# Linear attention into a tanh-shrink layer: inputs laid out as (head group, 64) x 9 tokens, q transposed by DMA, 1/den of batches 0 and 1 spread by fp32 matmuls, phi two batches ahead

## Chip, cores and metric

The kernel runs on one NeuronCore of one Trainium2 chip. The metric is the device time of one execution in microseconds (us); the median of three runs of the kernel before is 398.22 us (397.93 to 398.74). One execution was also recorded by the hardware profiler.

## What is computed

Shapes: q, k, v are (8 batches, 8 heads, 576 tokens, 64); the layer behind is 512 to 2048 to 512 over 4608 tokens.

```python
def _attn_ref(q, k, v):
    def phi(x):
        return np.where(x > 0, x, np.exp(x) - 1.0) + 1.0
    q_p, k_p = (phi(q), phi(k))
    kv = np.einsum('bhsd,bhse->bhde', k_p, v)
    z = np.sum(k_p, axis=2)
    num = np.einsum('bhsd,bhde->bhse', q_p, kv)
    den = np.einsum('bhsd,bhd->bhs', q_p, z)[..., None] + 1e-06
    return (num / den).astype(np.float32)

def _moe_ref(x, w_in, w_out):
    h = x @ w_in
    g = h - np.tanh(h)
    return (g @ w_out).astype(np.float32)
```

The attention output, laid out as 4608 tokens x 512, is the x of the second function.

## The kernel before

Everything is written in the order in which each engine is to run it (a manual schedule); engines wait for each other through semaphores only. Matmuls take bf16 operands; q, k, v and the weights are cast to bf16 by the loading DMAs, which GpSimd (POOL) issues.

The second layer is cut into nine **chunks** c of 512 tokens. In a chunk, L1 is sixteen calls of `l1` (4 matmuls of 512 columns into one PSUM bank h, a tanh on ScalarE (ACT), h - tanh(h) into gT on VectorE (DVE)); L2 is sixteen calls of `l2mm` (4 matmuls each into a bank o), and after every fourth an `evac` copies o to SBUF on ACT and SP stores it. `s1[fi]` and `s2[s]` are lists of attention steps that are emitted behind L1 step fi and L2 step s of a chunk; what stands there sets the order on all engines.

The attention of a **batch** has these steps. `a_kphi` and `a_qphi`: exp on ACT, max(x,0)+1 and the min of the two on DVE (tiles e, r, kp, qp). The 576 tokens lie as 512 (128 partitions x 4) and a rest of 64 with tiles of its own (km and kraw, qm and qraw, vm and vr), so phi runs twice. `a_qT`: twenty 128x128 transposes on TensorE (PE), four copies on ACT. `a_kv`: twenty matmuls of 192 columns, masked into kz by DVE. `a_den`: sixteen matmuls of 144 columns, then a reciprocal rden on DVE; rden goes to DRAM (ds) by four DMAs and comes back, copied to 64 partitions per head, as rdb by two more, all issued by SP. `a_num`: eight matmuls in five PSUM tiles, each multiplied by rdb on DVE into xT, the operand of L1.

`attention(0)` runs ahead of chunk 0 and `attention(1)` behind it, step after step, with no chunk beside them. From chunk 1 on, chunk c carries kv, den and num of batch c+1 (den at `s1[13]`, num from `s2[9]`) and phi and the transposes of batch c+2 (phi at `s2[0]` and `s2[1]`, transposes from `s2[3]`); chunk 1 carries phi and transposes of batch 2 as well. PSUM has six banks for h and o (pool dps) and two for all of attention (pool aps).

Of the kernel before, what the change touches and what calls it, by code (L numbers as in the profile page):

```python
# [15 lines left out]
def kernel(  # L16
# [51 lines left out]
    def load_k(b):
        km = kpool.tile([128, H, J, D], BF16, name="km")
        nc.gpsimd.dma_start(out=km.rearrange("p h j d -> p h (j d)"),  # L70
                            in_=k[b, :, 0:SM, :].rearrange("h (p j) d -> p h (j d)", j=J))
# [4 lines left out]
    def load_v(b):
        vm, vr = vm_b[b % 2], vr_b[b % 2]
        for p in range(NP):
            nc.gpsimd.dma_start(  # L79
                out=vm[:, p, 0:2].rearrange("p h j d -> p h (j d)"),  # L80
                in_=v[b, 2 * p:2 * p + 2, 0:SM, :].rearrange("h (p j) d -> p h (j d)", j=J))
# [5 lines left out]
    def load_q(b):
        qm = kpool.tile([128, H, J, D], BF16, name="qm")
        nc.gpsimd.dma_start(out=qm.rearrange("p h j d -> p h (j d)"),
                            in_=q[b, :, 0:SM, :].rearrange("h (p j) d -> p h (j d)", j=J))  # L90
        qr = kpool.tile([SR, H, D], BF16, name="qraw")
        nc.gpsimd.dma_start(out=qr, in_=q[b, :, SM:S, :].rearrange("h s d -> s h d"))
        qm_t[b], qrr_t[b] = qm, qr

    def load_w(g):
# [9 lines left out]
    kpm_t, qpm_t, qT_t, kz_t, rdb_t = {}, {}, {}, {}, {}  # L105

    def phi(src, dst):

        rows, n = src.shape[0], src.shape[1]
        e = work.tile([128, H, J, D], BF16, name="e")  # L110
        r = work.tile([128, H, J, D], BF16, name="r")
        ev, rv = (e, r) if len(src.shape) == 4 else (e[0:rows, :, 0, :], r[0:rows, :, 0, :])
        nc.scalar.activation(ev, src, AF.Exp)  # L113
        nc.vector.tensor_scalar(rv, src, 0.0, 1.0, ALU.max, ALU.add)
        nc.vector.tensor_tensor(dst, ev, rv, ALU.min)  # L115

    def a_phi(b, main, rem, persist, store, name):
        d = work.tile([128, J, H, D], BF16, name=name)
        phi(main[b], d.rearrange("p j h d -> p h j d"))
        phi(rem[b], persist[b % 2][0:SR])  # L120
        store[b] = d

    def a_kphi(b):
        a_phi(b, km_t, krr_t, kr_b, kpm_t, "kp")

    def a_qphi(b):
        a_phi(b, qm_t, qrr_t, qr_b, qpm_t, "qp")

    def a_qT(b, p):
        if p == 0:  # L130
            qT_t[b] = work.tile([128, NP, S], BF16, name="qT")
        qp, qr = qpm_t[b], qr_b[b % 2]
        ps = aps.tile([128, 1024], BF16, name="tps", tag="aps")
        for j in range(J):
            nc.tensor.transpose(ps[:, j * 128:(j + 1) * 128], qp[:, j, 2 * p:2 * p + 2, :], ident)  # L135
        nc.tensor.transpose(ps[:, SM:SM + 128], qr[:, 2 * p:2 * p + 2, :], ident)  # L136
        nc.scalar.copy(qT_t[b][:, p, :], ps[:, 0:S])  # L137

    def a_kv(b, half):
        if half == 0:  # L140
            kz_t[b] = work.tile([128, NP, 160], BF16, name="kz")
        kp, kr, vm, vr = kpm_t[b], kr_b[b % 2], vm_b[b % 2], vr_b[b % 2]
        ps = aps.tile([128, 2, 192], F32, name="kvps", tag="aps")
        for i in range(2):
            p = 2 * half + i
            for j in range(J):
                nc.tensor.matmul(ps[:, i, :], kp[:, j, 2 * p:2 * p + 2, :], vm[:, p, :, j, :],  # L147
                                 start=(j == 0), stop=False)
            nc.tensor.matmul(ps[:, i, :], kr[:, 2 * p:2 * p + 2, :], vr[:, p, :, :],
                             start=False, stop=True)  # L150
        nc.vector.tensor_mul(kz_t[b][:, 2 * half:2 * half + 2, :], ps[:, :, 0:160],
                             mask[:, 2 * half:2 * half + 2, :])

    def a_den(b):
        kz, qT = kz_t[b], qT_t[b]
        w = S // 4
        ps = aps.tile([128, w], F32, name="denps", tag="aps")
        for p in range(NP):
            for j in range(4):
                nc.tensor.matmul(ps[32 * j:32 * j + 32, :], kz[:, p, 128:160],  # L160
                                 qT[:, p, j * w:(j + 1) * w], start=(p == 0), stop=(p == NP - 1))
        den = rpool.tile([128, w], F32, name="den")
        nc.vector.tensor_scalar(den, ps, 1e-6, None, ALU.add)
        rden = rpool.tile([128, w], F32, name="rden")
        nc.vector.reciprocal(rden, den)
        ds = dram.tile([H, S], F32, name="ds")
        for j in range(4):
            nc.sync.dma_start(out=ds[:, j * w:(j + 1) * w], in_=rden[32 * j:32 * j + H, :])
        rdb = rpool.tile([128, NP, S], F32, name="rdb")
# [180 lines left out]
```

## Time and profile before

| | us |
|---|---|
| median of 3 runs | 398.22 |
| profiled execution, device time | 397.96 |
| its span in the trace | 396.2 |
| PE busy (share of the span) | 310.3 (78%) |
| DVE busy | 184.6 (47%) |
| ACT busy | 165.3 (42%) |
| POOL busy | 75.1 (19%) |
| chain of work that ended last: PE / DMA / DVE / ACT | 65% / 12% / 10% / 9% |

The page of the profile gives busy times, a map of the span in 40 slices, the DMA queues, the chain of work that ended last and the costliest groups of instructions. The trace behind it can be asked for a stretch of time, for the chain in order of time, and for groups kept apart by shape. A row of a group ends with the idle time of the engine ahead of it and with what ended that idle time ("<-DVE qp"). PEld is the loading of a stationary operand, which may lie beside matmuls.

### The profile page before, as it was taken

To read this page: it belongs to the slowest core of one execution; us is meant where nothing else is said; L and a number is where in the kernel's file an instruction comes from. 1 tells how busy PE (TensorE), PEld (TensorE's weight loads), DVE (VectorE), ACT (ScalarE), POOL (GpSimd) and SP (SyncE) were. 2 spreads that over 40 slices of the span, in tenths; PEclk is the share of its full clock that TensorE was granted. 3 is DMA by queue.
4 is the path that set the end of the run, shared out by engine and by line. 5 is a ranking of instruction groups with operands and counts; after the bars stand their busy time and mean duration, and the time that the engine had idled before them with its cause. 6 is when DMAs were issued, how large, how long until landed. Compare 5 with 4: busy or idle time off the path is not lost.

```text
span 396.2 us, 4437 instructions
## 1 busy us (share of the span) xinstructions
PE 310.3 (78%) x1664; PEld 148.3 (37%) x1664; DVE 184.6 (47%) x301; ACT 165.3 (42%) x245; POOL 75.1 (19%) x110
## 2 busy tenths in 40 slices
PE   0430888643359789969996999699969998999995
PEld 0310333231115344524452445244434544444442
DVE  6410522351266815781576258436823743640820
ACT  3310222542076733563456355526652631642731
POOL 8721650071031510340053005000000000000000
PEclk9855799965569989998998999899989999999999
DMA  9999994298374692269156905610062025001102
GB/s 112 173 206 227 170 149 46 80 137 125 66 88 51 96 208 86 33 103 215 57 59 138 179 34 61 148 54 26 4 146 73 9 48 155 26 28 54 25 28 79
DMA packets 49685, 37.66 MB, mean 95 GB/s; under 512 B 15104, under 2 KB 44032, under 8 KB 48640
## 3 DMA queue, kind: packets, MB, share of 16 engines
q0 software_dynamic: 42624, 18.36, 37.7%
q1 hardware_dynamic: 7040, 19.03, 17.1%
q8 instruction: 13, 0.21, 0.2%
q14 instruction: 8, 0.07, 0.1%
HBM read 46.14 MB, written 9.58 MB: 141 GB/s over the span
## 4 chain that ended last, share of the span: by engine, by line
PE 65%; DMA 12%; DVE 10%; ACT 9%; issue 2%; SPq 1%; POOL 0%; DVEq 0%; ACTq 0%; POOLq 0%
PE h L202 31%; PE o L210 25%; ACT e L113 6%; DMA rdb<-ds 6%; PE kvps L147 3%; DVE qp L115 2%; DVE kp L115 2%; DMA ds<-rden 2%; PE tps L135 2%; PE numps L181 2%; DMA km<-in_k_dram 2%; DMA qm<-in_q_dram 2%; DVE gT L206 1%; ACT th L205 1%; DVE xT L182 1%
## 5 line engine op out<-in xcount | busy, mean ns | idle before, releaser
L210 PE MATMUL o<-w_out_sb,gT 128*128 128x512 bf16 x576 | 142.7, 394 | 2.4 <-DVE gT L206 1.9
L202 PE MATMUL h<-xT,w_in_sb 128*128 128x512 bf16 x576 | 135.3, 389 | 2.2 <-DVE gT L206 1.6
L206 DVE TENSOR_TENSOR gT<-h,th 128x512 bf16<-128x512 f32 x144 | 98.6, 688 | 80.9 <-ACT th L205 80.9
L205 ACT ACTIVATE th<-h 128x512 f32<-128x512 f32 x144 | 86.0, 597 | 105.7 <-PE h L202 101.3
L210 PEld LDWEIGHTS <-gT 128*128 128x128 bf16 x576 | 56.5, 101 | 69.9 <-issue 6.2
L202 PEld LDWEIGHTS <-w_in_sb 128*128 128x128 bf16 x576 | 56.6, 100 | 69.2 <-issue 9.1
L182 DVE TENSOR_TENSOR xT<-numps,rdb 128x512 bf16<-128x512 f32 x32 | 21.6, 690 | 83.0 <-PE numps L181 47.2
L215 ACT COPY osb<-o 128x512 f32<-128x512 f32 x36 | 21.0, 583 | 74.7 <-PE o L210 73.4
L79 POOL DMA_DIRECT2D vm<-in_v_dram x32 | 22.6, 719 | 89.3 <-PE kvps L147 81.7
L135 PE MATMUL tps<-ident,qp 128*128 128x128 bf16 x128 | 15.3, 256 | 29.4 <-DVE qp L115 28.8
L181 PE MATMUL numps<-qT,kz 128*128 128x512 bf16 x32 | 13.6, 432 | 29.6 <-DVE xT L182 29.6
L137 ACT COPY qT<-tps 128x576 bf16<-128x576 bf16 x32 | 20.0, 639 | 30.9 <-PE tps L136 30.9
L147 PE MATMUL kvps<-vm,kp 128*128 128x192 bf16 x128 | 17.4, 276 | 15.5 <-DVE kp L115 15.5
L135 PEld LDWEIGHTS <-qp 128*128 128x128 bf16 x128 | 11.5, 117 | 40.3 <-DVE qp L115 32.5
L83 POOL DMA_DIRECT2D vr<-in_v_dram x32 | 19.3, 623 | 14.4 <-DMA w_out_sb<-in_moe_w_out_dram 8.5
L147 PEld LDWEIGHTS <-kp 128*128 128x128 bf16 x128 | 12.9, 109 | 19.0 <-DVE kp L115 16.0
L113 ACT ACTIVATE e<-qm 128x2048 bf16<-128x2048 bf16 x8 | 15.3, 1910 | 10.1 <-DMA qm<-in_q_dram 5.1
L70 POOL DMA_DIRECT2D km<-in_k_dram x8 | 7.3, 917 | 55.6 <-ACT e L113 54.0
L113 ACT ACTIVATE e<-km 128x2048 bf16<-128x2048 bf16 x8 | 15.2, 1904 | 5.5 <-DMA km<-in_k_dram 5.5
L181 PEld LDWEIGHTS <-kz 128*128 128x128 bf16 x32 | 3.0, 100 | 33.3 <-issue 30.2
L115 DVE TENSOR_TENSOR kp<-e,r 128x2048 bf16<-128x2048 bf16 x8 | 9.8, 1225 | 9.0 <-ACT e L113 9.0
L115 DVE TENSOR_TENSOR qp<-e,r 128x2048 bf16<-128x2048 bf16 x8 | 9.8, 1225 | 4.8 <-ACT e L113 4.6
(40 smaller groups left out, 123.1 us busy)
## 6 DMA issues: line engine op xcount, KB each, us to landing
rdb<-ds SPq DMA_DIRECT2D x16, 576.0 KB
out_dram<-osb SPq DMA_DIRECT2D x32, 256.0 KB
km<-in_k_dram POOLq DMA_DIRECT2D x8, 512.0 KB, 9.3
vm<-in_v_dram POOLq DMA_DIRECT2D x32, 128.0 KB, 4.2
qm<-in_q_dram POOLq DMA_DIRECT2D x8, 512.0 KB, 6.3
w_in_sb<-in_moe_w_in_dram POOLq DMA_DIRECT2D x4, 512.0 KB, 10.1
w_out_sb<-in_moe_w_out_dram POOLq DMA_DIRECT2D x4, 512.0 KB, 17.6
out_dram<-osb SPq DMA_DIRECT2D x8, 128.0 KB
```

Of the source, the lines that this page charges most:

```text
L79: nc.gpsimd.dma_start(out=vm[:, p, 0:2].rearrange("p h j d -> p h (j d)"), in_=v[b, 2 * p:2 * p + 2, 0:SM, :].rearrange("h (p j) d -> p h ...
L113: nc.scalar.activation(ev, src, AF.Exp)
L115: nc.vector.tensor_tensor(dst, ev, rv, ALU.min)
L135: nc.tensor.transpose(ps[:, j * 128:(j + 1) * 128], qp[:, j, 2 * p:2 * p + 2, :], ident)
L147: nc.tensor.matmul(ps[:, i, :], kp[:, j, 2 * p:2 * p + 2, :], vm[:, p, :, j, :], start=(j == 0), stop=False)
L181: nc.tensor.matmul(ps, kz[:, p, 0:128], qT[:, p, 0:SM], start=True, stop=True)
L182: nc.vector.tensor_mul(xT[:, p, cm:cm + SM], ps, rdb[:, p, 0:SM])
L202: nc.tensor.matmul(h, w_in_sb[:, p, fi * 128:(fi + 1) * 128], xT[:, p, c * 512:(c + 1) * 512], start=(p == 0), stop=(p == NP - 1))
L205: nc.scalar.activation(th, h, AF.Tanh)
L206: nc.vector.tensor_sub(gT[:, fi, :], h, th)
L210: nc.tensor.matmul(o, gT[:, fi, i * 128:(i + 1) * 128], w_out_sb[:, fi, :], start=(fi == 0), stop=(fi == NF - 1))
L215: nc.scalar.copy(osb, o)
```

## The change

All 576 tokens of a head now lie as 64 partitions x 9 consecutive tokens; heads 0 to 3 are on partitions 0 to 63 and heads 4 to 7 on 64 to 127 (hg is the half). The rest tiles and their work are gone. phi is called per half i of the heads, 1152 elements per partition. `a_kv` becomes 36 matmuls over 64 partitions each, the two halves in turn, into two PSUM tiles. For batches 2 to 7 q is transposed by one DMA from SP (`a_qT_dma`); batches 0 and 1 keep PE (`a_qT_pe`, copies split over ACT and DVE). For batches 0 and 1 rden no longer goes through DRAM: `a_num_direct` copies num to SBUF on ACT, spreads rden over partitions with 16 fp32 matmuls against a 0/1 tile `sel`, and multiplies on DVE. In chunk c from 1 on, kv of batch c+1 stands at `s1[6]`, den at `s1[10]`, num from `s2[8]`, and phi of batch c+2 at `s2[0]`, `s2[2]`, `s2[4]`, `s2[6]`, the DMA transpose behind it. Chunk 0 runs all of L1, then L2 with phi of batch 1 beside it. Each `evac` stores by two DMAs.

```diff
+    sel = const.tile([128, 4, NP, 2, 64], F32, name="sel")
...
+    def load_kq(b, src, store, name):
+        t = kpool.tile([128, 2, 2, J, D], BF16, name=name)
+        for hg in range(2):
+            nc.gpsimd.dma_start(
+                out=t[64 * hg:64 * hg + 64].rearrange("p i h j d -> p (i h) (j d)"),
+                in_=src[b, 4 * hg:4 * hg + 4].rearrange("h (p j) d -> p h (j d)", j=J))
...
+    def phi(b, src, store, name, i):
...
+        x = src[b][:, i]
+        e = work.tile([128, 2, J, D], BF16, name="e")
+        r = work.tile([128, 2, J, D], BF16, name="r")
+        nc.scalar.activation(e, x, AF.Exp)
+        nc.vector.tensor_scalar(r, x, 0.0, 1.0, ALU.max, ALU.add)
+        nc.vector.tensor_tensor(store[b][:, i].rearrange("p j h d -> p h j d"), e, r, ALU.min)
...
+    def a_qT_dma(b):
+        new_qT(b)
+        nc.sync.dma_start_transpose(
+            out=qT_t[b].rearrange("p i j g t -> p (i j) (g t)"),
+            in_=qp_t[b].rearrange("p i j h d -> p (i j h d)"))
...
+    def a_kv(b, pool, tag):
...
+        ps = [pool.tile([128, 2, 192], F32, name=f"kvps{hg}", tag=tag) for hg in range(2)]
         for i in range(2):
             for j in range(J):
+                for hg in range(2):
+                    r = slice(64 * hg, 64 * hg + 64)
+                    nc.tensor.matmul(ps[hg][:, i, :], kp[r, i, j].rearrange("p h d -> p (h d)"),
+                                     vt[r, i, :, j, :], start=(j == 0), stop=(j == J - 1))
...
+    def a_num_direct(b, pool, tag):
...
+        for p in range(NP):
+            ps = num_mm(b, p, pool, tag)
+            nc.scalar.copy(ns[:, p, 0:8, :], ps)
+        ps = num_mm(b, NP, pool, tag)
+        nc.scalar.copy(ns[:, :, 8, :], ps[:, 0:NP, :])
+        for p in range(NP):
+            for u in range(2):
+                bp = pool.tile([128, 2, J, 16], F32, name="bp", tag=tag)
+                for t in range(2):
+                    nc.tensor.matmul(bp[:, t].rearrange("p j c -> p (j c)"),
+                                     sel[:, 2 * u + t, p].rearrange("p h e -> p (h e)"), rden_t[b],
+                                     start=True, stop=True)
+                nc.vector.tensor_mul(
+                    xv(b, p)[:, 2 * u:2 * u + 2],
+                    ns[:, p].rearrange("p j (t c) -> p t j c", t=4)[:, 2 * u:2 * u + 2], bp)
...
+    load_k(0)
+    load_q(0)
+    load_v(0)
     make_identity(nc, ident)
+    nc.gpsimd.memset(sel, 0.0)
+    nc.gpsimd.affine_select(
...
     for g in range(4):
+        load_wi(g)
+    load_wo(0)
+    load_wo(1)
     load_k(1)
+    load_q(1)
+    load_wo(2)
+    load_wo(3)
     load_v(1)
...
+        a_kphi(0, i)
...
+        a_qphi(0, i)
...
+        a_qT_pe(0, i, dps, "dps")
+    a_kv(0, dps, "dps")
+    a_den(0, aps, "aps")
+    a_num_direct(0, dps, "dps")
...
+        if c >= 1 and n1 < B:
+            s1[6].append(lambda: a_kv(n1, aps, "aps"))
+            s1[10].append(lambda: (a_den(n1, aps, "aps"), a_spread(n1)))
             for p in range(NP + 1):
+                s2[8 + p].append(lambda p=p: a_num(n1, p))
+            if c + 3 < B:
+                s1[6].append(lambda: load_v(c + 3))
...
+                n2s = s2[0], s2[2], s2[4], s2[6]
+            n2s[0].append(lambda: a_kphi(n2, 0))
+            n2s[1].append(lambda: a_kphi(n2, 1))
+            n2s[2].append(lambda: a_qphi(n2, 0))
+            n2s[3].append(lambda: (a_qphi(n2, 1), a_qT_dma(n2)))
+            if c + 4 < B:
+                n2s[3].append(lambda: (load_k(c + 4), load_q(c + 4)))
...
+        if c == 0:
...
+                l2mm(gT, os_[i], i, 4 * g, 4 * g + 4)
...
+                if s < 12:
+                    for f in s2[s]:
+                        f()
+            for s in (12, 13):
+                s2[s][-1]()
+            a_kv(1, aps, "aps")
+            a_den(1, aps, "aps")
+            a_num_direct(1, aps, "aps")
...
+            for f in sum(n2s, []):
+                f()
+            continue
```

ACT at the seam between L1 and L2 of chunk 2, before (th is the tanh, e the exp of phi of batch 4, osb the copies of `evac`, tps the transposed q in PSUM):

```order
L205 ACTIVATE th<-h 128x512 x16
L113 ACTIVATE e<-km 128x2048
L113 ACTIVATE e<-kraw 64x8x64
L113 ACTIVATE e<-qm 128x2048
L113 ACTIVATE e<-qraw 64x8x64
L215 COPY osb<-o 128x512
L137 COPY qT<-tps 128x576 x4
L215 COPY osb<-o 128x512 x3
```

The same place with the change:

```order
L229 ACTIVATE th<-h 128x512 x16
L102 ACTIVATE e<-kraw 128x1152 x2
L239 COPY osb<-o 128x512
L102 ACTIVATE e<-qraw 128x1152 x2
L239 COPY osb<-o 128x512 x3
```

The four copies of the transposed q are gone from ACT, and one `evac` copy now stands between the exps of k and those of q.

SP in chunks 1 and 2, before (ds, rdb: the way of rden through DRAM; out_dram: the stores of `evac`):

```order
L168 DMA ds<-rden 8x144 x4
L171 DMA rdb<-ds 64x2304 x2
L217 DMA out_dram<-osb 64x512 x2
L217 DMA out_dram<-osb 128x512 x3
L168 DMA ds<-rden 8x144 x4
```

The same place with the change:

```order
L168 DMA ds<-rden 8x144 x4
L171 DMA rdb<-ds 64x2304 x2
L242 DMA out_dram<-osb 64x512 x2
L117 DMA_TRANSPOSE qT<-qp 128x18x128
L242 DMA out_dram<-osb 64x512 x6
L168 DMA ds<-rden 8x144 x4
```

The transpose stands behind the first store of a chunk and ahead of its other three, and it waits for qp from DVE.

DVE from the end of batch 1's attention into chunk 1, before (numps, rdb, xT: num times 1/den; gT: L1 of chunk 1; kp, qp: phi of batch 2):

```order
L165 RECIPROCAL rden<-den 128x144
L182 TENSOR_TENSOR xT<-numps,rdb 128x512 x4
L187 TENSOR_TENSOR xT<-numps,rdb 128x4x64
L206 TENSOR_TENSOR gT<-h,th 128x512
L114 TENSOR_SCALAR r<-km 128x2048
L115 TENSOR_TENSOR kp<-e,r 128x8x4x64
```

The same place with the change (ns is num in SBUF, bp the spread 1/den in PSUM):

```order
L161 RECIPROCAL rden<-den 128x144
L218 TENSOR_TENSOR xT<-ns,bp 128x2x9x16 x8
L103 TENSOR_SCALAR r<-kraw 128x1152
L104 TENSOR_TENSOR kp<-e,r 128x2x9x64
L103 TENSOR_SCALAR r<-kraw 128x1152
L104 TENSOR_TENSOR kp<-e,r 128x2x9x64
L103 TENSOR_SCALAR r<-qraw 128x1152
L104 TENSOR_TENSOR qp<-e,r 128x2x9x64
L103 TENSOR_SCALAR r<-qraw 128x1152
L104 TENSOR_TENSOR qp<-e,r 128x2x9x64
L230 TENSOR_TENSOR gT<-h,th 128x512 x7
```

All of phi of batch 2 moved from between the first subtractions of chunk 1 to ahead of them.

More of the change, by code (lines that the diff above doesn't have):

```diff
@@ L87, in load_q @@
[L87 to L95, printed above, removed]
+    v_b = [const.tile([128, 2, 3, J, D], BF16, name=f"v{i}") for i in range(2)]
@@ L96, in load_w, with load_wi @@
+    def load_wi(g):
         f0 = g * (DF // 4)
@@ L102, in load_wo @@
                             in_=moe_w_out[512 * g:512 * g + 512, :].rearrange("(ko ki) f -> ki ko f", ki=128))
[L105 to L137, printed above, removed]
@@ L155, in a_den @@
+    def a_den(b, pool, tag):
         kz, qT = kz_t[b], qT_t[b]
-        w = S // 4
-        ps = aps.tile([128, w], F32, name="denps", tag="aps")
+        ps = pool.tile([128, J, 16], F32, name="denps", tag=tag)
         for p in range(NP):
[L159 to L169, printed above, removed]
+            for t in range(4):
+                nc.tensor.matmul(ps[32 * t:32 * t + 32], kz[:, p, 128:160],
+                                 qT[:, p % 2, :, p // 2, 16 * t:16 * t + 16],
+                                 start=(p == 0), stop=(p == NP - 1))
```

220 lines of the change are left out of this document (101 added, 119 removed).

## The prediction

> **What bounds the kernel now.** I read the busy times by stage first: each row is a stretch in us from the span's start, its length, then busy time (and instructions) of PE, PEld, DVE, ACT and POOL, the granted PE clock, the DMA share and GB/s.
>
> ```profile
> 78.00:106.76 28.76, 8.99 (x64) 5.51 (x65) 9.74 (x16) 7.70 (x9) 8.38 (x12) 0.58 0.76 120
> 106.76:154.40 47.64, 39.19 (x213) 18.78 (x213) 25.65 (x41) 25.23 (x35) 12.43 (x16) 0.86 0.70 104
> 154.40:192.08 37.68, 33.86 (x193) 16.50 (x192) 20.95 (x33) 19.08 (x28) 8.56 (x12) 0.95 0.61 107
> ...
> 267.42:305.02 37.60, 33.78 (x194) 16.55 (x192) 20.95 (x33) 19.08 (x28) 0.00 (x0) 0.95 0.23 60
> 305.02:336.96 31.94, 30.89 (x174) 14.86 (x172) 15.89 (x25) 11.90 (x20) 0.00 (x0) 1.00 0.26 72
> 336.96:364.59 27.63, 27.63 (x129) 12.54 (x128) 11.07 (x16) 11.90 (x20) 0.00 (x0) 1.00 0.10 39
> ```
>
> Chunk 7 (the last row) carries no attention: 27.63 us, PE full, 27.63/128 = 0.216 us per matmul of 512 columns. Chunks 2 to 5 take 150.6 us in all (154.40 to 305.02), 10 us more each; chunk 1 takes 20 more; chunk 6, which has kv, den and num but neither phi nor transposes, 4.3 more. DVE and ACT are busy for 21 and 19 of 37.7 us: neither is a bound. The stretch behind chunk 0 is nearly PE-free. So the kernel is PE plus holes. The chain that ended last shows the hole of a steady chunk (chunk 2), and the timeline who waited:
>
> ```profile
> 170.86 1.91 ACT e L113
> 172.79 1.24 DVE kp L115
> 174.05 1.92 ACT e L113
> 176.00 1.23 DVE qp L115
> ```
>
> ```profile
> 177.28 0.40 PE L135 MATMUL tps<-ident,qp 128*128 128x128 bf16 x4 [3.50 <-DVE qp L115]
> ```
>
> PE runs out of L2 work and waits 3.5 us for qp, since its transposes stand behind `s2[3]`. Around batches 0 and 1 the same chain shows:
>
> ```profile
> 1.43 6.06 DMA km<-in_k_dram
> ...
> 29.60 9.86 DMA rdb<-ds
> ...
> 42.07 5.05 PE h L202 x16
> ...
> 75.22 2.88 DMA out_dram<-osb
> ...
> 83.77 0.64 PE kvps L147 x4
> ...
> 85.41 0.49 DVE kz L151
> ...
> 91.19 0.88 PE denps L160 x13
> ...
> 92.43 1.06 DVE rden L165
> ...
> 96.36 7.24 DMA rdb<-ds
> ```
>
> L1 of chunk 0 starts at 42.07, L1 of chunk 1 at 106.76; ahead of both the end is set by 1/den on its way through DRAM.
>
> **Steady chunks (2 to 5).** The 20 transposes and four ACT copies go; phi has no PE reader within its chunk any more. PE keeps the GEMM, kv, den and num. The rows, from chunks 2 and 6:
>
> ```profile
> 163.28 0.49 PE L147 MATMUL kvps<-vm,kp 128*128 128x192 bf16 x4
> ...
> 163.69 1.89 PE L202 MATMUL h<-xT,w_in_sb 128*128 128x512 bf16 x8
> ```
>
> ```profile
> 318.69 0.43 PE L160 MATMUL denps<-qT,kz 128*32 128x144 bf16 x16
> ...
> 332.05 1.89 DVE L182 TENSOR_TENSOR xT<-numps,rdb 128x512 bf16<-128x512 f32 x3 [9.49 <-DMA rdb<-ds]
> ```
>
> Five kv matmuls take 163.69 - 163.28 = 0.41 us, 0.082 each. The 36 over half the partitions cost 36 x 0.082 = 2.95 us in series. If the halves run side by side they cost half, 1.5: the den row shows four column groups doing so, 16 matmuls in 0.43 us, 0.027 each, far under 0.082. I take the middle, **2.2**. With den 0.4 and num 4 x 0.216 + 0.3 = 1.2, PE's work is 27.63 + 2.2 + 0.4 + 1.2 = **31.4 us**. (Check on chunk 6: 27.63 + 20 x 0.082 + 0.4 + 1.2 = 30.9, PE busy 30.89; the other 1.07 is the wait for rdb.)
>
> That wait: in chunk 6 rdb landed 332.05 - 318.69 = 13.4 us after den began. With the change PE reaches the third num tile, the first that needs a bank back from DVE, 0.4 + 14 x 0.864 + 2 x 1.08 = 14.7 us after den (a group of four matmuls is 0.864); the first multiply (0.69) would end at 14.1. That fits by 0.6. In chunks 1 to 4 the v load falls into this stretch, so I charge 0.5: **31.9** there, 31.4 in chunks 5 and 6. Phi itself lies beside L2: DVE does 4 x 1.2 us and ACT 4 x 1.15 and four copies in 13.8 us (the lines for 1152 elements are worked out below).
>
> **The DMA transpose** has no row in this trace. It moves 128 x 2304 x 2 = 589,824 bytes. The nearest row is the software queue's:
>
> ```profile
> q0 software_dynamic: 42624, 18.36, 37.7%
> ```
>
> 37.7% of 16 engines x 396.2 us over 42,624 packets is 56 ns of one engine per packet. In rows of 256 bytes (one block's row) it is 2304 packets x 56 / 16 = **8.1 us**, which I take; the low end is nothing. In chunks 2 on it has cover: qp is done about 7.3 us into L2 (the last tanh, four exps and a copy, then a min), its reader den comes 6.5 + 1.2 us of L2 and num, 9.5 of L1 and 2.2 of kv later, 19.4 us. Queued behind it on SP are three stores, whose osb buffers have a chunk of slack, then the next ds. In chunk 1 there is less: phi of batch 2 ends 4.8 us after L1 starts and den comes at 12.0, cover 7.2, so 0.9 us shows. The Trainium skill (Advanced Engine Details and Errata, X-Bar Transpose (TRN2)) says that transposing DMAs are as fast as ordinary ones and expects 350 to 400 GB/s; by that, an estimate of 1.7 us, the 0.9 goes. The same page (DGE: Hardware vs Software) calls the hardware generator, which SP uses, the worse one at transposes; no run here shows either.
>
> **Start to L1 of chunk 0.** Rows kept apart by shape:
>
> ```profile
> L182 DVE TENSOR_TENSOR xT<-numps,rdb 128x512 bf16<-128x512 f32 x32 | 21.6, 690 | 83.0 <-PE numps L181 47.2 <-DMA rdb<-ds 35.6
> ...
> L113 ACT ACTIVATE e<-km 128x2048 bf16<-128x2048 bf16 x8 | 15.2, 1904 | 5.5 <-DMA km<-in_k_dram 5.5
> L115 DVE TENSOR_TENSOR kp<-e,r 128x2048 bf16<-128x2048 bf16 x8 | 9.8, 1225 | 9.0 <-ACT e L113 9.0
> ...
> L114 DVE TENSOR_SCALAR r<-km 128x2048 bf16<-128x2048 bf16 x8 | 5.5, 684 | 0.3 <-DMA km<-in_k_dram 0.3
> L113 ACT ACTIVATE e<-kraw 64x512 bf16<-64x512 bf16 x8 | 4.9, 616 | 0.0
> ...
> L187 DVE TENSOR_TENSOR xT<-numps,rdb 128x256 bf16<-128x256 f32 x8 | 3.4, 422 | 1.7 <-PE numps L186 1.7
> L115 DVE TENSOR_TENSOR kr<-e,r 64x512 bf16<-64x512 bf16 x8 | 3.3, 418 | 0.8
> ...
> L114 DVE TENSOR_SCALAR r<-kraw 64x512 bf16<-64x512 bf16 x8 | 2.2, 278 | 0.0
> ```
>
> Straight lines through 512 and 2048 elements give, at 1152, exp 1.15, min 0.75, max/add 0.45 us; the line through L187 and L182 gives 0.46 at 288. The page's line of what the DMAs moved, in 40 slices of 9.9 us:
>
> ```profile
> GB/s 112 173 206 227 170 149 46 80 137 125 66 88 51 96 208 86 33 103 215 57 59 138 179 34 61 148 54 26 4 146 73 9 48 155 26 28 54 25 28 79
> ```
>
> k and q together are 1.18 MB in bf16; the first slice's 112 GB/s brings them in by 10.4 us, v at 173 GB/s by 13.8. exp of q's halves ends at 11.6 and 12.7, the last min at 13.5, nine transposes (0.16 each, as the cold kv matmuls, 0.64 for four) at 14.9. kv cold is 36 x 0.16 = 5.8 in series, 2.9 in pairs; 4.3 taken: 19.2. Two kz (0.49 each) and den (0.88): 21.1; den's add and reciprocal: 22.5; num, with cold matmuls of 5.05/16 = 0.32, 1.7 us: 22.8.
>
> Then the **16 fp32 matmuls**, 144 columns each, which no row shows. Low end: one cold bf16 matmul, 0.16. [...] I take the middle, **0.6**, 9.6 us, ahead of DVE's 8 x 0.46; with the last multiply L1 starts at **32.9** instead of 42.07. The Trainium skill (FP8 and Floating Point Precision, TensorE Precision Notes) counts four passes for true fp32; 4 x 0.16 = 0.64, an estimate, would add 0.6 us per batch.
>
> POOL now builds sel ahead of w_in's loads:
>
> ```profile
> 0.74 0.20 POOL masks.py:197 MEMSET ident<- 128x128 bf16 x1 [0.29 <-POOLq L334]
> ...
> 1.02 0.29 POOL masks.py:199 TENSOR_SCALAR_AFFINE_SELECT ident<-ident 128x128 bf16<-128x128 bf16 x1
> ...
> 18.23 0.89 POOL L70 DMA_DIRECT2D km<-in_k_dram  x1 [1.51 <-DMA w_in_sb<-in_moe_w_in_dram]
> ...
> 25.83 0.71 POOL L79 DMA_DIRECT2D vm<-in_v_dram  x1 [1.84 <-DMA w_in_sb<-in_moe_w_in_dram]
> ```
>
> sel has 16 times the elements: at most 16 x 0.49 = 7.9 us. Its end is then 15.3, and with 2.5 us per w_in load (18.23 to 25.83 is three) the last lands near 28, still under 32.9. Nothing is charged.
>
> **Chunk 0 and batch 1.** Chunk 0 in one piece is 27.63 + 0.8 (half of what the first 16 matmuls now lose, 5.05 - 3.45): 61.3. phi of batch 1 lies beside its L2. Then, with two PSUM banks only: the fourth `evac` waits for a store (2.88) and holds ACT for 1.6 us, the transposes with their copies, two banks in turn, end 4.3 us after L2 by my estimate, kv 4.3, kz and den 1.9, rden 1.4, first bp 0.9 later, 9.6 for the fp32 matmuls, 0.5 for the last multiply: 22.9. Chunk 1 starts at **84.2** instead of 106.76. Phi of batch 2 stands ahead of chunk 1's first subtraction on DVE, 4.8 us; six banks of h cover 5.2, so 0.3 shows. Chunk 1 is 31.9 + 0.3 + 0.9 = 33.1 instead of 47.64, where phi of two batches stood.
>
> **Sum.** 84.2 + 33.1 + 3 x 31.9 + 2 x 31.4 = 275.8 at the start of chunk 7; the rest as before, 396.2 - 336.96 = 59.2, plus 0.3 for the last store in two DMAs: 335.3. The profiled run took 397.96 for its 396.2, so **337.1**. That run is 0.07% under the median of 398.22.
>
> **Rivals.** *Dear or cheap matmuls*: fp32 at 1.0 adds 2 x 16 x 0.4 = 12.8, at 0.16 takes 14.1 away; kv in series or in pairs is 0.7 for each of six chunks and 1.45 twice, 7 either way. Together 357 or 316.
>
> *A half-slow transpose*: at d us it costs d - 8.1 more in chunk 1 and d - 19.4 in each of five chunks beyond 19.4; d = 16 (128-byte packets) gives 345, d = 20 gives 352.
>
> *Slower than before*: the transpose cut into short packets. The gain is 60.9; it is gone when (d - 8.1) + 5 (d - 19.4) exceeds it, from **d = 28** on. With 64-byte packets d = 32.3: 337 + 24 + 65 = 426; with 32-byte packets d = 64.6: about 620. For it: the 56 ns are a mean over packets of 18.36 MB / 42,624 = 430 bytes, so a cut into shorter ones costs in proportion to their number, and no row shows how a transpose is cut. Against it: nothing in the layout asks for it, a block's row is 256 contiguous bytes on both sides.
>
> *The steady gain does not come*: the rdb wait takes the hole's place. It would need rdb some 6 us later than in chunk 6; the slowest rdb of the chain took 9.86 where 7.24 was seen too, so 2.6 is covered by a row and 6 is not. Chunks 2 to 5 would stay at 37.65 and the time would be 361.
>
> **Chances.** Forecast (326 to 348) 0.55; cheap 0.12; dear 0.10; half-slow transpose 0.12; slower 0.08; no steady gain 0.03. The range 320 to 358 takes in all of the first, most of cheap and dear and half of the half-slow transpose, 0.8. About 0.2% is what a measurement can tell from no change. Faster 0.91, same 0.01, slower 0.08.
>
> **What would show it.** Right: L1 of chunk 0 near 33 and of chunk 1 near 84, no wait of PE for qp, chunks 2 to 5 near 31.9, den not waiting for qT but briefly in chunk 1. Wrong: PE waiting at den for the transpose, the 16 bp matmuls over 16 us or under 3, kv over 3 us warm, multiplies waiting for rdb in every chunk.

## The result, and the profile after

The changed kernel takes **334.38 us** (median of 4 runs, 332.12 to 334.82) against 398.08 (397.24 to 398.74) for the kernel before: a ratio of 0.8389 with a 95% interval of 0.8348 to 0.8431. The forecast was 337.1, in a range of 320 to 358. The profiled execution spans 333.1 us, where the forecast's sum gave 335.3. This agreement is luckier than it looks: the terms of the sum miss by up to 11.7 us, in both directions.

The page's first lines after the change (busy us and share of the span) and its line of the chain that ended last:

```profile
span 333.1 us, 4536 instructions
...
PE 292.0 (88%) x1702; PEld 144.5 (43%) x1732; DVE 184.7 (55%) x303; ACT 149.9 (45%) x227; POOL 49.9 (15%) x80
...
PE 77%; DMA 11%; DVE 5%; ACT 2%; issue 2%; SPq 1%; POOL 0%; DVEq 0%; ACTq 0%; POOLq 0%
```

PE's busy time fell only from 310.3 to 292.0 us; of the 63 us gained in the span the rest, some 45, is holes. (A slow clock counts as busy time: the mean granted clock was 0.901 before and is 0.974 now, so part of the 18 is clock.) Where the holes were is read from busy times by chunk (stretch, length, busy time of PE, PEld, DVE, ACT, POOL, granted PE clock, DMA share, GB/s), for chunks 0, 1, 2, 3, 6 and 7:

```profile
26.52:73.78 47.26, 40.86 (x238) 22.90 (x240) 22.49 (x40) 22.10 (x33) 12.37 (x20) 0.93 0.95 167
73.78:118.55 44.77, 32.49 (x184) 14.99 (x187) 25.50 (x42) 17.52 (x25) 7.29 (x12) 0.89 0.89 125
118.55:149.33 30.78, 30.47 (x186) 14.54 (x189) 20.79 (x33) 16.11 (x24) 4.85 (x8) 1.00 0.70 134
149.33:180.37 31.04, 30.77 (x186) 14.53 (x188) 20.60 (x33) 16.11 (x24) 4.84 (x8) 1.00 0.83 154
242.00:272.77 30.77, 30.46 (x185) 14.52 (x188) 16.10 (x25) 11.89 (x20) 0.00 (x0) 1.00 0.30 74
272.77:300.40 27.63, 27.52 (x128) 12.51 (x129) 11.07 (x16) 11.89 (x20) 0.00 (x0) 1.00 0.17 39
```

From chunk 2 on PE is full to within 0.3 us. Chunk 1 is 14 us longer than a steady chunk although it holds the same PE work; the forecast for it was 33.1. (The first stretch includes batch 1's attention behind chunk 0.) Step by step, in us:

| stretch | forecast | measured | error |
|---|---|---|---|
| start to L1 of chunk 0 | 32.9 | 26.5 | -6.4 |
| chunk 0 and batch 1 | 51.3 | 47.3 | -4.0 |
| chunk 1 | 33.1 | 44.8 | +11.7 |
| chunks 2 to 4 | 95.7 | 92.7 | -3.0 |
| chunks 5 and 6 | 62.8 | 61.55 | -1.25 |
| chunk 7 to the end | 59.5 | 60.3 | +0.8 |
| span | 335.3 | 333.1 | -2.2 |

**The start.** PE's timeline after the change (start, length, what, count, and in brackets the wait ahead of it):

```profile
14.35 1.14 PE L127 MATMUL tps<-ident,qp 128*128 128x128 bf16 x9 [14.35 <-DVE qp L104]
...
16.91 2.73 PE L143 MATMUL kvps<-v,kp 64*128 64x192 bf16 x36
20.22 0.70 PE L155 MATMUL denps<-qT,kz 128*32 128x144 bf16 x16 [0.58 <-DVE kz L146]
...
22.52 4.16 PE L215 MATMUL bp<-rden,sel 128*128 128x144 f32 x32 [0.51 <-DVE rden L161]
26.52 3.67 PE L226 MATMUL h<-xT,w_in_sb 128*128 128x512 bf16 x15
```

The 16 fp32 matmuls (32 records) begin at 22.52, where the forecast had 22.8, and take 4.16 us where it had 9.6: **0.26 us each, not 0.6**. The start is met only because two errors cancel. The last transposes of q end at 17.0 and not at 14.9: the last min on DVE ends at 15.8 instead of 13.5, behind ACT's table load of 1.28 us, which now comes only when k has landed, and behind DVE's first two steps, which took 1.45 and 1.63 us. The 36 kv matmuls then take 2.73 us instead of 4.3.

**Behind chunk 0.** ACT's and then PE's timeline:

```profile
53.54 0.58 ACT L239 COPY osb<-o 128x512 f32<-128x512 f32 x1 [0.28 <-PE o L234]
58.62 0.58 ACT L239 COPY osb<-o 128x512 f32<-128x512 f32 x1 [4.50 <-DMA out_dram<-osb]
```

```profile
59.85 0.38 PE L127 MATMUL tps<-ident,qp 128*128 128x128 bf16 x4 [4.03 <-ACT qT L131]
60.45 3.27 PE L143 MATMUL kvps<-v,kp 64*128 64x192 bf16 x36 [0.21 <-ACT qT L131]
...
67.48 6.24 PE L215 MATMUL bp<-rden,sel 128*128 128x144 f32 x32
73.78 5.19 PE L226 MATMUL h<-xT,w_in_sb 128*128 128x512 bf16 x23
...
97.26 0.67 PE L155 MATMUL denps<-qT,kz 128*32 128x144 bf16 x16 [11.10 <-DMA qT<-qp]
97.86 5.84 PE L226 MATMUL h<-xT,w_in_sb 128*128 128x512 bf16 x19
```

The fourth `evac` copy waits 4.50 us for a store to give its osb buffer back (forecast 1.6), ACT's copy of the transposed q stands behind it, and PE waits 4.03 for that. In chunk 1 the last row but one is the large miss: PE waits **11.10 us** at den for the DMA transpose of batch 2. Behind it 19 matmuls take 5.84 us, 0.31 each instead of 0.216.

The chain in order of time has the two transfers:

```profile
53.03 5.49 DMA out_dram<-osb
...
79.41 17.72 DMA qT<-qp
```

The transpose was issued at 79.41, nearly as early as forecast (5.6 us after L1 of chunk 1 starts, 4.8 forecast), and landed 17.72 us later, not 8.1. POOL's timeline shows what went out beside it, the k, q and v loads of batch 4 (k and q follow batch 2's phi, v follows its kv; 0.59 MB each in bf16):

```profile
76.35 0.62 POOL L64 DMA_DIRECT2D kraw<-in_k_dram  x1 [10.63 <-issue]
77.14 0.61 POOL L64 DMA_DIRECT2D kraw<-in_k_dram  x1 [0.16 <-issue]
78.99 1.22 POOL L64 DMA_DIRECT2D qraw<-in_q_dram  x2 [1.25 <-ACT th L229]
82.15 2.51 POOL L79 DMA_DIRECT2D v<-in_v_dram  x4 [1.94 <-PE kvps L143]
```

Two theories follow. **Contention**: a transpose alone is as cheap as forecast, and is slow here since it shares the DMA engines with loads that the same code triggers. **Cost of its own**: it takes 16 us or so anywhere, and chunk 1 only lacks the cover. That no later chunk waits does not tell them apart, since the cover there is 19.4 us. The DMA share already leans to the first: the transposes of batches 6 and 7, which have no loads beside them, were issued at 203.75 and 234.60, and by 211.0 and 242.0, 7.3 and 7.4 us later, all DMA engines are idle.

### The profile page after: what moved, and what is told of

Same layout as the page of the kernel before. It is cut to its first block, busy times and chain, and to the rows that moved or that the text cites. A ratio compares the mean times of both kernels' runs of the same rounds, so it can differ in the third digit from the quotient of the medians.

```text
span 333.1 us, 4536 instructions
## 1 busy us (share of the span) xinstructions
PE 292.0 (88%) x1702; PEld 144.5 (43%) x1732; DVE 184.7 (55%) x303; ACT 149.9 (45%) x227; POOL 49.9 (15%) x80
## 4 chain that ended last, share of the span: by engine, by line
PE 77%; DMA 11%; DVE 5%; ACT 2%; issue 2%; SPq 1%; POOL 0%; DVEq 0%; ACTq 0%; POOLq 0%
PE o L234 34%; PE h L226 34%; DMA qT<-qp 5%; PE kvps L143 4%; PE bp L215 3%; DMA rdb<-ds 3%; DMA out_dram<-osb 2%; DMA kraw<-in_k_dram 2%; PE numps L180 2%; DVE r L103 1%; DVE qp L104 1%; PE denps L155 1%; DVE kp L104 1%; ACT ns L208 1%; DVE rden L161 1%
## 5 line engine op out<-in xcount | busy, mean ns | idle before, releaser
L234 PE MATMUL o<-w_out_sb,gT 128*128 128x512 bf16 x564 | 129.8, 379 | 0.8
L239 ACT COPY osb<-o 128x512 f32<-128x512 f32 x36 | 21.1, 585 | 88.1 <-PE o L234 80.7
L79 POOL DMA_DIRECT2D v<-in_v_dram x32 | 19.2, 612 | 63.9 <-PE kvps L143 56.7
L194 DVE TENSOR_TENSOR xT<-numps,rdb 128x512 bf16<-128x512 f32 x24 | 16.2, 690 | 18.7 <-DMA rdb<-ds 11.1
L102 ACT ACTIVATE e<-qraw 128x1152 bf16<-128x1152 bf16 x16 | 18.1, 1161 | 6.8 <-DVE kp L104 6.6
L127 PE MATMUL tps<-ident,qp 128*128 128x128 bf16 x36 | 3.8, 265 | 19.2 <-DVE qp L104 14.7
L102 ACT ACTIVATE e<-kraw 128x1152 bf16<-128x1152 bf16 x16 | 17.7, 1155 | 0.0
L143 PE MATMUL kvps<-v,kp 64*128 64x192 bf16 x288 | 16.0, 269 | 0.7 <-ACT qT L131 0.2
L143 PEld LDWEIGHTS <-kp 64*128 64x128 bf16 x288 | 13.9, 105 | 3.3 <-issue 3.1
L104 DVE TENSOR_TENSOR qp<-e,r 128x1152 bf16<-128x1152 bf16 x16 | 12.1, 758 | 5.5 <-ACT e L102 4.4
L155 PE MATMUL denps<-qT,kz 128*32 128x144 bf16 x128 | 4.1, 241 | 12.4 <-DMA qT<-qp 11.1
L104 DVE TENSOR_TENSOR kp<-e,r 128x1152 bf16<-128x1152 bf16 x16 | 13.0, 813 | 3.0 <-ACT e L102 1.0
L215 PE MATMUL bp<-rden,sel 128*128 128x144 f32 x64 | 10.3, 321 | 0.7 <-DVE rden L161 0.5
```

Source lines behind the costliest of these rows:

```text
L79: nc.gpsimd.dma_start(out=v_b[b % 2][64 * hg:64 * hg + 64, i, 0:2].rearrange("p h j d -> p h (j d)"), in_=v[b, h0:h0 + 2].rearrange("h (p ...
L102: nc.scalar.activation(e, x, AF.Exp)
L104: nc.vector.tensor_tensor(store[b][:, i].rearrange("p j h d -> p h j d"), e, r, ALU.min)
L143: nc.tensor.matmul(ps[hg][:, i, :], kp[r, i, j].rearrange("p h d -> p (h d)"), vt[r, i, :, j, :], start=(j == 0), stop=(j == J - 1))
L215: nc.tensor.matmul(bp[:, t].rearrange("p j c -> p (j c)"), sel[:, 2 * u + t, p].rearrange("p h e -> p (h e)"), rden_t[b], start=True, stop ...
L234: nc.tensor.matmul(o, gT[:, fi, i * 128:(i + 1) * 128], w_out_sb[:, fi, :], start=(fi == 0), stop=(fi == NF - 1))
```

## The experiments

Each ratio is to the kernel before on the same chip (398.4 to 398.9 us), and each edit is against the changed kernel, whose four executions lie between 332.1 and 334.8 us. Chunk lengths are from one profiled execution of each run.

### Batch 2 transposed by PE

```diff
+            if n1 == 2:
+                s1[7].append(lambda: a_qT_pe(2, 0, aps, "aps"))
+                s1[8].append(lambda: a_qT_pe(2, 1, aps, "aps"))
...
-            n2s[3].append(lambda: (a_qphi(n2, 1), a_qT_dma(n2)))
+            n2s[3].append(lambda: a_qphi(n2, 1))
+            if n2 > 2:
+                n2s[3].append(lambda: a_qT_dma(n2))
```

> The changed kernel with q of batch 2 alone transposed by matmuls on PE (18 of them behind L1 steps 7 and 8 of chunk 1) in place of the DMA; batches 3 to 7 keep the DMA. Theory (chunk 1 is long because den waits 11.1 us for the DMA transpose, and PE then starts at half clock): chunk 1 falls from 44.8 us to about 33.5 (11.1 and 1.7 of clock go, 18 matmuls of about 0.09 us come), the time to about 324. Rival (something else holds chunk 1, the copies of qT or the 1/den transfers): less than 4 us gained, above 330.

Measured: **323.68 us** (323.11 to 323.95), ratio 0.8115 (0.8098 to 0.8133); chunk 1 took 33.69 us. PE in chunk 1:

```profile
83.73 0.78 PE L127 MATMUL tps<-ident,qp 128*128 128x128 bf16 x9 [0.40 <-DVE kz L146]
...
85.21 0.67 PE L127 MATMUL tps<-ident,qp 128*128 128x128 bf16 x9
...
87.54 0.43 PE L155 MATMUL denps<-qT,kz 128*32 128x144 bf16 x16
```

Den no longer waits, 18 transposes cost 1.45 us, and L1 keeps its speed behind it. The transpose of this one batch by DMA cost 10.7 us of the changed kernel's time.

### The loads of batch 4 held back

POOL is made to wait for 1/den of batch 2 before it issues the loads of batch 4; nothing else competes with the transpose of batch 2 then.

```diff
+    def hold():
+        held = mpool.tile([128, 1], F32, name="held")
+        nc.gpsimd.tensor_copy(held, rden_t[2][:, 0:1])
...
-            if c + 3 < B:
+            if c + 3 < B and c > 1:
...
+            if c == 1:
+                s1[10].append(lambda: (hold(), load_k(4), load_q(4), load_v(4)))
...
-            if c + 4 < B:
+            if c + 4 < B and c > 0:
```

> The changed kernel with the DMA transpose of batch 2 as it is, but the loads of k, q and v of batch 4 held back on POOL until rden of batch 2 is there, that is, until the transpose has landed. Theory A (the transpose took 17.7 us because it shares the DMA engines with 1.77 MB of loads): it lands in 6 to 9 us, den waits under 3 us, chunk 1 near 35 us, the time near 326. Theory B (17.7 us are the transpose's own): den waits 10 us or more again and the time stays within 2 us of 334.

Measured: 329.41 us (325.97 to 329.9), ratio 0.8242 (0.8198 to 0.8287); chunk 1 took 40.07 us, so theory A holds for the transpose and misses the chunk's length and the time. SP's issue of the transpose, PE at den and num of batch 2, and the busy times between issue and den:

```profile
78.96 2.49 SPq L117 DMA_TRANSPOSE qT<-qp  x1
```

```profile
85.64 0.43 PE L155 MATMUL denps<-qT,kz 128*32 128x144 bf16 x16
...
106.08 0.58 PE L180 MATMUL numps<-qT,kz 128*128 128x512 bf16 x1 [5.66 <-DVE xT L194]
```

```profile
78.96:85.64 6.68, 6.11 (x57) 3.21 (x57) 6.33 (x12) 4.29 (x8) 0.00 (x0) 1.00 0.47 88
```

The transpose landed within 6.68 us, so den didn't wait: **contention it is**. In that stretch the DMAs moved 6.68 us x 88 GB/s = 0.59 MB, just the transpose's bytes, at a share of 0.47, so they were busy for 6.68 x 0.47 = 3.1 us with it; taken by half us, they moved up to 217 GB/s and were idle from 83.5 on, so it had landed some 4.5 us after its issue. Contention costs more than the two transfers in a row would: in the run above, without this transpose, the same loads kept the engines busy for some 10.5 us (77.3 to 87.8), here the transpose alone did so for 3.5 (80.0 to 83.5), and together they took some 20 in the changed kernel (77.4 to 97.1). Why they slow each other so is open.

The cost didn't vanish, it moved: the held loads now run beside 1/den on its way through DRAM, which the chain shows as

```profile
89.44 3.95 DMA ds<-rden
...
94.08 11.13 DMA rdb<-ds
```

and num waits 5.66 us for rdb instead. The next transpose's issue kept SP for 12.66 us.

### All of q transposed by PE

`a_qT_pe` for batches 2 to 7, at `s1[7]` and `s1[8]` as above, with no DMA transpose left.

```diff
+            s1[7].append(lambda: a_qT_pe(n1, 0, aps, "aps"))
+            s1[8].append(lambda: a_qT_pe(n1, 1, aps, "aps"))
...
-            n2s[3].append(lambda: (a_qphi(n2, 1), a_qT_dma(n2)))
+            n2s[3].append(lambda: a_qphi(n2, 1))
```

> q of batches 2 to 7 is transposed by TensorE (behind s1[7] and s1[8] of the chunk ahead), none by DMA. Theory: a DMA transpose saves TensorE 1.6 to 2.0 us in each later chunk and costs time in chunk 1 alone. Then chunk 1 is 33 to 34 us as in the run with batch 2 alone on TensorE, chunks 2 to 6 are 32.4 to 32.8 us instead of 30.8, and the time is 331 to 334 us. Rival: the DMA transposes save nothing (the PE transposes fit where TensorE waits anyway); then chunks 2 to 6 stay at 30.8 and the time is 324.

Measured: **329.12 us** (327.79 to 329.97), ratio 0.8252 (0.8223 to 0.8281). Chunk 1 took 33.48 us, chunks 2 to 6 took 32.03 to 32.12. The time is below the expected 331 to 334: a DMA transpose saves 1.2 us per later chunk, 6 in all, less than expected, and loses 11 in chunk 1: **all six together made the change some 5 us slower than PE would have been**. The two runs also give a transpose's price on the DMA engines. The hardware queue after the change, and here without transposes (packets, MB, share of 16 engines' span):

```profile
q1 hardware_dynamic: 21120, 20.17, 28.4%
```

```profile
q1 hardware_dynamic: 7104, 16.63, 20.4%
```

Six transposes are 14,016 packets, 2336 each (2304 forecast), and 0.284 x 333.1 - 0.204 x 326.0 = 28.1 us of all 16 engines. If all of that difference is the transposes', they cost **4.7 us each** by this estimate, loads beside them, 32 ns per packet instead of 56.

### 1/den back through DRAM

```diff
-    a_num_direct(0, dps, "dps")
+    a_spread(0)
+    for p in range(NP + 1):
+        a_num(0, p)
...
-            a_num_direct(1, aps, "aps")
+            a_spread(1)
+            for p in range(NP + 1):
+                a_num(1, p)
```

> 1/den of batches 0 and 1 goes back through DRAM as in the kernel before, all else as after. Theory: at the seams into chunk 0 and chunk 1 nothing but kv hides the way through DRAM (7 to 10 us each, with the loads on the same queues), so the time rises by 8 to 16 us less the fp32 matmuls' 4.2 and 6.2 us taken out: 340 to 350 us. Rival: the matmuls were no cheaper than the way through DRAM; then 333 to 336 us.

Measured: 352.03 us (350.37 to 355.38), ratio 0.884 (0.8787 to 0.8892): the fp32 spread is worth **17.7 us**, a little more than the theory's upper end. PE's two waits:

```profile
40.51 1.18 PE L180 MATMUL numps<-qT,kz 128*128 128x512 bf16 x2 [18.46 <-DVE xT L194]
...
91.45 1.18 PE L180 MATMUL numps<-qT,kz 128*128 128x512 bf16 x2 [13.39 <-DVE xT L194]
```

L1 of chunk 0 starts at 42.47 instead of 26.52: nearly all of the spread's worth lies at the start, where ds and rdb (4.48 and 10.73 us in the chain) run beside the weight loads (which POOL issues on a queue of its own, over the same 16 engines). Behind chunk 0 only 3.7 us were gained, since there the fp32 matmuls, at 6.24 us, and the store's hold stand against the way through DRAM.

### Phi back in the chunk's second half

```diff
+            if n1 == 2:
+                s1[7].append(lambda: a_qT_pe(2, 0, aps, "aps"))
+                s1[8].append(lambda: a_qT_pe(2, 1, aps, "aps"))
...
-                n2s = s2[0], s2[2], s2[4], s2[6]
+                n2s = s2[0], s2[0], s2[1], s2[1]
...
-            n2s[3].append(lambda: (a_qphi(n2, 1), a_qT_dma(n2)))
+            n2s[3].append(lambda: a_qphi(n2, 1))
+            if c > 0:
+                s2[3].append(lambda: a_qT_pe(n2, 0, aps, "aps"))
+                s2[5].append(lambda: a_qT_pe(n2, 1, aps, "aps"))
```

> phi of the next batch is back at the chunk's second half (s2[0], s2[1]) and q is transposed by TensorE at s2[3] and s2[5], the data laid out as after. Theory: TensorE's wait for qp at the seam (3.5 to 4 us) comes back and the transposes' 1.7 us with it: chunks 2 to 6 take 35.5 to 37 us, and the time is 350 to 365 us. Rival: what made the steady chunks shorter is the 9-token layout alone (kv and num in fewer, larger matmuls); then chunks 2 to 6 are at 32.5 and the time is near 333.

Measured: 337.39 us (336.05 to 338.47), ratio 0.846 (0.843 to 0.8491); chunks 2 to 5 took 33.78, 33.79, 33.61 and 33.61. Neither expectation holds: the hole is back, but half as long as before the change. PE in chunk 3, and that chunk's busy times:

```profile
163.79 0.68 PE L127 MATMUL tps<-ident,qp 128*128 128x128 bf16 x9 [1.84 <-DVE qp L104]
```

```profile
142.36:176.15 33.79, 31.74 (x203) 15.49 (x206) 21.54 (x35) 17.48 (x26) 4.84 (x8) 1.00 0.59 119
```

With the run that has all of q on PE this splits a steady chunk's gain. Means of chunks 2 to 5: 37.66 before, 33.70 in this run (new layout, phi and transposes where they were), 32.06 with phi spread over L2 and q transposed by PE in the next chunk, 30.86 after the change. **The new layout, with kv, den and num at their new places, brought 4.0 us per chunk, the removal of the qp wait 1.6, the DMA transpose 1.2.** Of the 4.0, the hole's first half is 3.50 - 1.84 = 1.7. PE's busy time is 2.1 less (33.8 to 31.7), but that is hardly less work: the clock was 0.95 on average before and is 1.00 here, which by 0.05 x 37.7 is an estimate of 1.9 us. Behind the hole of 3.50 us the clock fell to 0.50 (at 179 to 181 us in the kernel before), where four matmuls of L2 took 1.72 us (at 178.06) and four others 1.03 once it was back (at 182.03); behind the hole of 1.84 it stayed at 1.00. The hole itself is shorter since the first transposes now need only half of q: from the first exp to them it took 4.75 us (159.04 to 163.79), before 6.42 (170.86 to 177.28).

### kv without neighbours in different row halves

```diff
-            for j in range(J):
-                for hg in range(2):
-                    r = slice(64 * hg, 64 * hg + 64)
+            for hg in range(2):
+                r = slice(64 * hg, 64 * hg + 64)
+                for j in range(J):
```

> The 36 kv matmuls of a batch in another order: all of one row half before the other, so that neighbours use the same rows. Theory: neighbours in different row halves overlap (0.046 us each); without, 36 take 2.95 us (0.082 each) instead of 1.6, so chunks 2 to 6 are 1.3 us longer and the time is 342 to 345 us. Rival: the halves don't overlap and the price is set by the columns alone; then the time stays at 334.

Measured: 337.76 us (335.38 to 338.65), ratio 0.8479 (0.8448 to 0.851). kv in chunk 3 after the change, then here:

```profile
155.47 1.66 PE L143 MATMUL kvps<-v,kp 64*128 64x192 bf16 x36
```

```profile
153.84 2.21 PE L143 MATMUL kvps<-v,kp 64*128 64x192 bf16 x36
```

Both expectations miss: the order is worth 0.55 us per batch, neither 1.3 nor nothing, and chunks 2 to 6 are longer by as much (31.3 to 31.5 us). Without alternating halves a matmul takes 2.21/36 = 0.061 us, less than the 0.082 of the kernel before, whose matmuls used all 128 rows; with them 0.046. What makes 64-row matmuls cheaper in a row is open.

### Four osb buffers

```diff
+    opool = ctx.enter_context(tc.tile_pool(name="opool", bufs=4))
...
-        osb = mpool.tile([128, DM], F32, name="osb")
+        osb = opool.tile([128, DM], F32, name="osb")
```

> The changed kernel with four buffers for osb in place of three. Theory (the fourth store copy of chunk 0 waits on ACT until a store has landed, 58.6 us, and the transposes of batch 1 stand behind it): PE's wait at the transposes of batch 1 falls from 4.0 us to under 1, chunk 1 starts 3 to 4 us earlier, the time is 330 to 331. Rival (the store's landing is waited for elsewhere too, or ACT is busy anyway): under 1 us.

Measured: **325.46 us** (324.16 to 327.18), ratio 0.8151 (0.8126 to 0.8176). PE behind chunk 0 and in chunk 1 (line numbers are one higher):

```profile
56.77 1.66 PE L144 MATMUL kvps<-v,kp 64*128 64x192 bf16 x36 [0.56 <-ACT qT L132]
...
62.24 5.23 PE L216 MATMUL bp<-rden,sel 128*128 128x144 f32 x32 [0.21 <-ACT ns L209]
67.31 5.40 PE L227 MATMUL h<-xT,w_in_sb 128*128 128x512 bf16 x24
...
88.57 0.67 PE L156 MATMUL denps<-qT,kz 128*32 128x144 bf16 x16 [8.67 <-DMA qT<-qp]
```

The time is below the theory's 330 to 331. Chunk 0 and batch 1 took 40.62 us instead of 47.26; in the runs with three buffers and the fp32 spread it was 46.0 to 47.6. That is more than the wait of 4.0: kv fell from 3.27 to 1.66 and the fp32 matmuls from 6.24 to 5.23, since PE's granted clock stayed at 1.00 without the wait (0.74 to 0.77 on average with it). The transpose in chunk 1 took 15.29 us here, so its wait fell too, to 8.67; that need not come from the buffers, as the other runs below 17.72 show.

### sel built behind the loads

sel's memset and select move behind the loads of k of batch 1; a one-column exp at the start loads ACT's table early. Both changes are in one run, so it can't tell them apart.

```diff
-    nc.gpsimd.memset(sel, 0.0)
-    nc.gpsimd.affine_select(
...
     for g in range(4):
         load_wi(g)
     load_wo(0)
     load_wo(1)
     load_k(1)
+    nc.gpsimd.memset(sel, 0.0)
+    nc.gpsimd.affine_select(
...
+    warm = const.tile([128, 1], F32, name="warm")
+    nc.scalar.activation(warm, mask[:, 0, 0:1], AF.Exp)
```

> The changed kernel with sel built on POOL after the loads of k of batch 1 in place of ahead of the weight loads, and one exp on a single column at the start, which brings the activation table in while the loads run. Theory (the table load of 1.28 us and the slow DVE instructions while POOL builds sel, 1.45 in place of 0.45 and 1.63 in place of 0.76, are on the path to L1 of chunk 0): L1 of chunk 0 starts 2 to 3 us earlier (26.5 to about 24), the time about 332. Rival (q's load sets the time, its max/add began at 12.7 us after waiting): under 1 us.

Measured: 330.19 us (328.66 to 331.53), ratio 0.8279 (0.8243 to 0.8316). L1 of chunk 0 starts at 25.72, 0.8 us earlier, as the rival has it; in the six profiled executions that leave the start alone it lies between 26.05 and 26.69, so a part of even that may be chance. k landed about 1 us later beside w_in's loads and took most of the gain back. DVE's first steps after the change and here:

```profile
7.42 1.45 DVE L103 TENSOR_SCALAR r<-kraw 128x1152 bf16<-128x1152 bf16 x1 [2.56 <-DMA kraw<-in_k_dram]
9.88 1.63 DVE L104 TENSOR_TENSOR kp<-e,r 128x1152 bf16<-128x1152 bf16 x1 [1.01 <-ACT e L102]
```

```profile
8.41 0.46 DVE L103 TENSOR_SCALAR r<-kraw 128x1152 bf16<-128x1152 bf16 x1 [2.85 <-DMA kraw<-in_k_dram]
9.59 0.76 DVE L104 TENSOR_TENSOR kp<-e,r 128x1152 bf16<-128x1152 bf16 x1 [0.72 <-ACT e L102]
```

DVE's two steps are short again, as forecast. Not every step of DVE is slowed beside POOL: sel is now filled from 15.30 to 19.40 us, and DVE's copy of the transposed q at 15.89 takes 0.42 us, as in the changed kernel without it.

In the profiled execution the rest of the gain lies in chunk 0 with batch 1 (1.2 us) and in chunk 1 (4.2 us), where the transpose landed in 13.68 us and den waited 7.07. That this comes from the edit is not shown: in the five profiled executions that issue the transpose in chunk 1 beside the loads, it landed in 13.68 to 17.72 us, and in the one with another order of kv, which has sel where it was, in 14.32.

### The three together

Batch 2 on PE, four osb buffers and the late sel, each edit as shown.

> Batch 2 of q transposed by TensorE, four osb buffers, and sel built behind the loads, together. Theory: the three remove different waits (den's 11.1 us at batch 2, tps's 4.0 us in chunk 0, DVE's 1 us at the start), so 334.4 less 10.7, 6.5 and about 1 gives 314 to 318 us. Rival: what four osb buffers gained in chunk 1 was partly the same wait (den's fell by 2.4 us there); then 318 to 321 us.

Measured: **314.8 us** (314.47 to 315.29), ratio 0.7906 (0.7889 to 0.7923), faster than both kernels. Busy times from L1 of chunk 0 to the end of chunk 2:

```profile
24.54:65.16 40.62, 37.85 (x241) 20.02 (x238) 22.40 (x39) 22.12 (x33) 12.02 (x20) 1.00 1.10 199
65.16:98.86 33.70, 32.28 (x209) 15.56 (x207) 25.93 (x45) 18.80 (x27) 7.29 (x12) 1.00 0.78 139
98.86:129.63 30.77, 30.77 (x190) 14.55 (x188) 20.79 (x33) 16.11 (x24) 4.85 (x8) 1.00 0.78 148
```

The theory's 314 to 318 holds. Alone the three gained 10.7, 8.9 and 4.2 us, 23.8 in all, together 19.6: in the profiles of the other two, made alone, the wait at den, which the first removes, was 2.4 and 4.0 us shorter already.

## Why the prediction was right, and where it was wrong

- **What bounds the kernel** (PE plus holes; DVE and ACT no bound) was right. The holes it named are the ones that went, with 1.9 us of slow clock behind the hole of a steady chunk that it had not seen, and the steady chunks now lie within 0.3 us of PE's work.
- **Steady chunks**, 31.9 and 31.4 forecast, 30.8 to 31.0 measured. The 0.5 charged for rdb was too much: apart from small waits it fits. kv, taken as 2.2 between 1.5 and 2.95, is 1.66; even without pairs it is 2.21, so the upper end, from the old rows of 128 partitions, was no price for these matmuls. That the hole for qp would go was right; the phi run shows that the new layout had halved it already.
- **Start to L1 of chunk 0**: the times up to the fp32 matmuls are met to 0.5 us (kv done at 19.2 forecast, 19.6 measured; den 21.1 and 20.9), but by luck: phi and the transposes of q ended 2.1 us late and kv was 1.6 us cheaper. The term mis-sized is the 16 fp32 matmuls: 9.6 forecast, 4.16 measured. Their price was built on 0.16 us for a cold bf16 matmul, read where PE's clock was 0.50 (at 83.77 in the kernel before); in this stretch the clock row reads 1.00. No run shows the 1.0 us of the dear rival, or a price near it: it was 0.26 here, 0.33 with two PSUM banks and 0.39 at the low clock. By the steady rate, 0.216 us for 512 columns, one pass of 144 columns is 0.061, and 0.26 is 4.3 such passes. The Trainium skill (FP8 and Floating Point Precision, TensorE Precision Notes) counts four passes for true fp32, and the measured 0.26 is near that count. Whether the passes set the price is not shown, since 32 weight loads fill 3.94 of the 4.16 us beside them.
- **Chunk 0 and batch 1**: the same term again (9.6 forecast, 6.24 at the low clock, 5.23 at the full one) and kv (4.3 and 3.27) came out cheaper. Against that the store's hold was 4.5 us, not 1.6: the forecast took the 2.88 us of a store of before, and here it took 5.49. The four-buffer run shows what the hold costs, clock included.
- **Chunk 1**, 33.1 forecast, 44.8 measured, is the step that failed: "queued behind it on SP" was looked at, and what shares the DMA engines with it was not. The 8.1 us supposed that the transpose has all 16 engines to itself; its own work is indeed below that (2336 packets, 4.7 us with loads beside it, 3.1 with hardly any), and it lands within 6.7 us once the loads are held. Among the loads it took 17.72. So 11.1 us of wait instead of 0.9, and some 1.7 us more because the clock fell behind the wait (19 matmuls in 5.84 us instead of 19 x 0.216 = 4.1). With batch 2 on PE the chunk takes 33.69. The half-slow rival had the right duration, d = 16 to 20, with another cause (short packets): at 17.72 its sum puts 0.9 + 9.6 = 10.5 us of wait into chunk 1, near the 11.10 measured, and 347 us for the whole. The Trainium skill (Advanced Engine Details and Errata, X-Bar Transpose (TRN2)) holds transposing DMAs to be as fast as ordinary ones; worked out from its bandwidth, the estimate was 1.7 us. No run here shows 1.7; 3.1 us of all engines is the lowest, at up to 217 GB/s.
- **The rivals**: the slower one fell, as packets are rows of 256 bytes after all. No steady chunk waited for a transpose. "Cheap" was half right: the first two stretches came out 10.4 us shorter, mostly by them, and chunk 1 took 11.7 back. The total was met because these two cancel.

## What to carry to other kernels

A transfer moved onto the DMA engines must be priced with what else is on them at that moment, and first of all with the loads that the same step releases: the cheap place for it is where it has cover to spare, and the one batch without cover (here batch 2) is better left to the engine that did it before. A wait of PE can cost more than its length: behind those of 3.50 us and more that were looked at here the matmuls ran at a lower clock for some us, behind one of 1.84 they did not. So a buffer more, which removes a wait of 4 us, can bring 6.6. When a total is met, compare the terms as well: here two misses of over 10 us (the first two stretches together, and chunk 1) cancelled, and the larger one pointed at a kernel 20 us faster.

## What the runs showed of the hardware

- During a wait of PE of 11.10 us the granted clock fell to 0.50 and stayed there until some 4 us after it; 19 matmuls took 0.31 us each on average instead of 0.216. Behind a wait of 4.03 us it was 0.74 to 0.77 on average for 13 us, behind one of 3.50 us it fell to 0.50 for some 3 us, and behind one of 1.84 us it stayed at 1.00, as in the four-buffer run, whose waits at batch 1 are all under 0.6 us.
- The same DMA transpose of 0.59 MB landed in 13.68 to 17.72 us beside 1.77 MB of loads and in at most 6.68 us alone (the DMA share says some 4.5). Its issue kept SP's queue for 2.49 us alone, 5.36 beside the loads, and 12.66 once.
- At the start nine transposes took 1.14 us, later 0.67, and 36 kv matmuls 2.73 against 1.66, although the clock row reads 1.00 in both places. Why is open.
- While POOL filled sel, DVE's two steps of phi beside it took 1.45 and 1.63 us; with sel moved away 0.46 and 0.76. A copy out of PSUM beside the moved sel took 0.42 us, no longer than without.
- An fp32 matmul shows as two records and two weight loads of 0.19 us with records of their own; 16 of them took 4.16 us with six PSUM banks in turn and 5.23 with two, both at full clock.
